# Moving two elementwise passes of a backward pass's last phase to GpSimd and its running sums to ScalarE

## The chip, the cores and the metric

The kernel runs on one core of a Trainium2 chip. The metric is the device time of one execution in microseconds (us). The kernel before takes 434.45 us, the median of three runs (434.1 to 438.83). Runs of one kernel wander by about 1%, so each kernel below is compared with runs of the kernel before on the same chip, in the same rounds.

Names used throughout: PE is TensorE, DVE is VectorE, ACT is ScalarE, POOL is GpSimd, SP is SyncE, which issues the DMAs. L1231 is line 1231 of the kernel's source. The change has one line less than the kernel before, so the same statement can carry a number one lower there.

## The reference, cut to what matters

A transformer block with a spectral mixing layer (a 2D FFT filter) and a squared-ReLU MLP, both behind a modulated layer norm, is run forward and backward in bf16. All gradients are outputs.

```python
def _layernorm(x, axis=-1, eps=1e-05):
    m = jnp.mean(x, axis=axis, keepdims=True)
    v = jnp.var(x, axis=axis, keepdims=True)
    return (x - m) / jnp.sqrt(v + eps)
# ... in the forward function:
    h = _layernorm(x, axis=-1) * (1 + ca) + sa
    x = x + ga * _A_ref(h, A_w_r, A_w_i)          # spectral layer
    h = _layernorm(x, axis=-1) * (1 + cb) + sb
    x = x + gb * _B_ref(h, B_w1, B_b1, B_w2, B_b2) # MLP
# ... and jax.vjp of it for the gradients
```

The last phase computes the gradient through the first layer norm for 2048 rows of 512. For a row with normalised value n and incoming gradient h, it needs h\*n summed over the rows (for the modulation), and two sums along the row, of s and of s\*n, where s is the scaled gradient. Beside that, TensorE still computes the gradient of the MLP's second weight.

## The kernel before

The 2048 rows are 16 tiles of 128, taken in 8 pairs. One pair does this:

```python
def row_pair(t, Ts):
    n1, gxl = rows3[t]                      # loaded from DRAM, two buffers each
    ...                                     # gh1, q1: three buffers; gn, gs, rr: two
    for i in range(2):
        psY = spec_g3(tc, K, Ts[i], psE)    # PE
        nc.scalar.copy(out=gs[:, i, :], in_=psY)                       # L1226
    unfold(nc, fp, gh1, gs, 2, "unf_u")     # four DVE passes, L261 to L265
    nc.vector.tensor_tensor(gn, gh1, modb[:, CA1_B, None, :].broadcast_to([P, 2, D]), op=ALU.mult)  # L1228
    for i in range(2):
        nc.scalar.activation(gs[:, i, :], gn[:, i, :], AF.Copy, scale=inv1[...], accum_out=rr[:, i, 0:1])  # L1230
    nc.vector.tensor_tensor(q1, gh1, n1, op=ALU.mult)                  # L1231
    late.add(lambda: colsums1(t, gh1, q1))  # PE sums over rows, L1212, 4 to 7 us after q1 in the trace, under 2 us for the last two pairs
    for i in range(2):                      # product and running sum in one, L1235
        jk = fp.tile([P, D], BF16, name="jk1", bufs=1)
        nc.vector.scalar_tensor_tensor(out=jk, in0=gs[:, i, :], scalar=K["onef"], in1=n1[:, i, :],
                                       op0=ALU.mult, op1=ALU.mult, accum_out=rr[:, i, 1:2])
    nc.vector.tensor_scalar(rr[:, :, 2:4], rr[:, :, 0:2], -1.0 / D, None, op0=ALU.mult)   # L1237
    for i in range(2):
        nc.vector.tensor_scalar(gn[:, i, :], n1[:, i, :], rr[:, i, 3:4], rr[:, i, 2:3], ...)  # L1239
    nc.vector.tensor_tensor(gs, gn, gs, op=ALU.add)                    # L1240
    gx = fp.tile([P, 2, D], BF16, name="gx")
    nc.vector.tensor_tensor(gx, gs, gxl, op=ALU.add)                   # L1242
    nc.sync.dma_start(out1_view[:, t:t + 2, :], gx)
    load_rows3(t + 4)
```

Between the pairs stand units of the weight gradient, each 16 matmuls, an evacuation from PSUM on DVE, an output, and a transposing load for a later unit:

```python
def grad_w2(fc):
    ps = mmps.tile([P, SB], FP32, name="mm")
    for t in range(NT):
        nc.tensor.matmul(ps, lhsT=hns[fc][:, t, :], rhs=g_sb[:, t, :], ...)   # L1150
    gw = gwp.tile([P, D], BF16, name="gw", bufs=3)
    with tc.high_priority():
        nc.vector.tensor_tensor(gw, ps, modb[:, GB_B, :], op=ALU.mult)        # L1153
    nc.sync.dma_start(out6_view[:, fc, :], gw)
    load_hn()                                                                 # L1145, transposing
```

## Time and profile before

| | before |
|---|---|
| time, median | 434.45 us |
| span of the profiled run | 436.5 us |
| row phase: start of the first unfold pass to end of the last gx | 358.94 to 424.80, 65.9 us |
| DVE busy in the row phase | 57.3 us |
| PE gaps longer than 0.1 us, from the first unfold to the last matmul | 7.4 us |
| GpSimd work in the row phase | none |

The row phase is the stage to read. The share of a whole run says little about it: from 359 to 425 PE is busy for 58.63 and DVE for 57.47 of 66 us, the DMA share is 1.03, and GpSimd is idle. The prediction shows the lines.

### The profile page before, as it was taken

To read this page: it belongs to the slowest core of one execution; us is meant where nothing else is said; L and a number is where in the kernel's file an instruction comes from. 1 tells how busy PE (TensorE), PEld (TensorE's weight loads), DVE (VectorE), ACT (ScalarE), POOL (GpSimd) and SP (SyncE) were. 2 spreads that over 40 slices of the span, in tenths; PEclk is the share of its full clock that TensorE was granted. 3 is DMA by queue.
4 is the path that set the end of the run, shared out by engine and by line. 5 is a ranking of instruction groups with operands and counts; after the bars stand their busy time and mean duration, and the time that the engine had idled before them with its cause. 6 is when DMAs were issued, how large, how long until landed. Compare 5 with 4: busy or idle time off the path is not lost.

```text
span 436.5 us, 7027 instructions
## 1 busy us (share of the span) xinstructions
PE 398.5 (91%) x2353; PEld 195.4 (45%) x2375; DVE 351.4 (80%) x846; ACT 261.2 (60%) x493; POOL 13.0 (3%) x64
## 2 busy tenths in 40 slices
PE   2789989999999999999999999999899799993996
PEld 0335446654444434443444444455455464441332
DVE  6887758959997588969897998909686968978896
ACT  5797889769881286348536765365348375445331
POOL 6120000000000000000000000000000000000000
PEclk9998999999999999999999999999999999999899
DMA  8995779999298469669965997987995699999984
GB/s 240 238 291 146 188 290 267 279 311 256 91 379 245 136 114 352 165 165 229 270 195 153 222 338 267 211 204 229 273 300 158 168 253 259 222 260 244 275 235 144
DMA packets 149738, 101.09 MB, mean 232 GB/s; under 512 B 98753, under 2 KB 135494, under 8 KB 149062
## 3 DMA queue, kind: packets, MB, share of 16 engines
q1 hardware_dynamic: 149138, 100.12, 86.6%
q10 hardware_dynamic: 564, 0.53, 0.4%
q8 instruction: 18, 0.29, 0.3%
q14 instruction: 18, 0.15, 0.1%
HBM read 35.44 MB, written 41.60 MB: 176 GB/s over the span
## 4 chain that ended last, share of the span: by engine, by line
PE 35%; DVE 28%; DMA 14%; ACT 12%; SPq 5%; issue 5%; POOL 1%; ACTq 0%; DVEq 0%
PE og L880 10%; PE mm L853 6%; PE mm L694 4%; PE mm L1150 4%; DMA n<-n_dram 3%; DMA out_dram<-gw 2%; DMA x<-in_A_x_dram 2%; DVE gm_junk L465 2%; PE psG L341 2%; SPq L1145 2%; PE mod_ps L595 2%; PE mm L1081 2%; DMA n_dram<-x_sb 2%; DVE l_st L795 1%; ACT r L855 1%
## 5 line engine op out<-in xcount | busy, mean ns | idle before, releaser
L694 PE MATMUL mm<-gT,w2T 128*128 128x512 bf16 x224 | 58.1, 383 | 3.4 <-DVE gab L697 2.7
L853 PE MATMUL mm<-h2T,w 128*128 128x512 bf16 x224 | 53.6, 379 | 1.7 <-ACT r L855 1.5
L1150 PE MATMUL mm<-g_sb,hn 128*128 128x512 bf16 x217 | 51.6, 387 | 3.8 <-DVE gw L1153 3.4
L1081 PE MATMUL mm<-gab,h_sb 128*128 128x448 bf16 x256 | 51.5, 352 | 2.5 <-ACT gw L1085 2.5
L880 PE MATMUL og<-w1T,gab 128*128 128x512 bf16 x218 | 49.9, 379 | 1.1 <-DVE o L945 0.8
L880 PE MATMUL og<-w,h 128*128 128x512 bf16 x217 | 49.1, 379 | 0.3
L855 ACT ACTIVATE r<-mm,b1col 128x512 bf16<-128x512 f32 x56 | 37.0, 684 | 6.1 <-PE mm L853 3.7
L1081 PEld LDWEIGHTS <-h_sb 128*128 128x128 bf16 x256 | 24.6, 98 | 24.2 <-issue 3.6
L853 PEld LDWEIGHTS <-w 128*128 128x128 bf16 x224 | 21.1, 97 | 30.6 <-issue 8.8
L1150 PEld LDWEIGHTS <-hn 128*128 128x128 bf16 x224 | 21.3, 99 | 29.8 <-issue 7.1
L880 PEld LDWEIGHTS <-h 128*128 128x128 bf16 x224 | 21.8, 98 | 26.1 <-issue 0.9
L880 PEld LDWEIGHTS <-gab 128*128 128x128 bf16 x224 | 21.6, 98 | 25.9 <-issue 1.4
L694 PEld LDWEIGHTS <-w2T 128*128 128x128 bf16 x224 | 20.9, 98 | 23.1 <-issue 6.5
L893 ACT CAST G<-og 128x512 bf16<-128x512 f32 x16 | 9.2, 580 | 27.9 <-PE og L880 27.9
L699 ACT CAST gab<-mm 128x512 bf16<-128x512 f32 x36 | 21.7, 602 | 3.0 <-PE mm L694 2.9
L857 DVE TENSOR_TENSOR h<-r 128x1024 bf16<-128x1024 bf16 x28 | 19.2, 687 | 4.8 <-ACT r L855 4.8
L1085 ACT CAST gw<-mm 128x448 bf16<-128x448 f32 x16 | 8.7, 543 | 24.0 <-DMA out_dram<-gw 15.0
L1230 ACT ACTIVATE gs<-gn,inv 128x512 bf16<-128x512 bf16 x16 | 11.4, 716 | 18.3 <-DVE gn L1228 18.3
L413 DVE TENSOR_TENSOR p<-Z,G 128x1028 bf16<-128x1028 bf16 x8 | 5.6, 697 | 19.9 <-DMA Xb<-xs_dram 11.6
L372 ACT ACTIVATE Tsb<-psT 128x512 bf16<-128x512 f32 x32 | 18.5, 604 | 1.6 <-PE psT L370 1.6
L465 DVE SCALAR_TENSOR_TENSOR gm_junk<-wmc,onef,gmbc 128x512 bf16<-128x512 bf16 x24 | 17.9, 747 | 1.9 <-DMA wmc<-in_w_mod_dram 1.0
L697 DVE CAST gab<-mm 128x512 bf16<-128x512 f32 x20 | 13.7, 686 | 6.8 <-PE mm L694 6.7
(287 smaller groups left out, 757.1 us busy)
## 6 DMA issues: line engine op xcount, KB each, us to landing
h_dram<-h SPq DMA_DIRECT2D x28, 256.0 KB, 3.6
gh_dram<-gab SPq DMA_DIRECT2D x28, 256.0 KB, 3.8
w<-in_B_w_dram SPq DMA_DIRECT2D x2, 1792.0 KB, 7.7
wmc<-in_w_mod_dram SPq DMA_DIRECT2D x12, 256.0 KB, 4.7
out_dram<-gwm SPq DMA_DIRECT2D x12, 256.0 KB, 3.7
wz_dram<-Z SPq DMA_DIRECT2D x8, 258.0 KB, 2.4
xs_dram<-Xs SPq DMA_DIRECT2D x8, 258.0 KB, 3.2
Z<-wz_dram SPq DMA_DIRECT2D x8, 258.0 KB, 4.3
```

What stands on the lines that cost most here:

```text
L372: nc.scalar.activation(Tsb, ps, AF.Copy, scale=EF_S)
L465: nc.vector.scalar_tensor_tensor(out=junk, in0=wmc[:, i, :], scalar=K["onef"], in1=gmbc, op0=ALU.mult, op1=ALU.mult, accum_out=self.gsc[:, ...
L694: nc.tensor.matmul(ps, lhsT=w2T[:, dc, fc * P:(fc + 1) * P], rhs=gT[b][:, :, dc, :], start=(dc == 0), stop=(dc == 3))
L697: nc.vector.tensor_copy(out=gaT[b][:, fc, :], in_=ps)
L699: nc.scalar.copy(out=gaT[b][:, fc, :], in_=ps)
L853: nc.tensor.matmul(ps, lhsT=w1[:, dc, (fc + i) * P:(fc + i + 1) * P], rhs=h2T[b][:, :, dc, :], start=(dc == 0), stop=(dc == 3))
L855: nc.scalar.activation(r[:, i, :], ps, AF.Relu, bias=b1col[:, fc + i:fc + i + 1])
L857: nc.vector.tensor_tensor(h2, r, r, op=ALU.mult)
L880: nc.tensor.matmul(ps, lhsT=lhs(fc), rhs=rhs[:, fc, :], start=(fc == 0), stop=(fc == NFC - 1))
L1081: nc.tensor.matmul(ps[:, 0:W4], lhsT=h2_sb[:, t, dc * P:(dc + 1) * P], rhs=ghn[t // 4][:, t % 4, fs], start=(t == 0), stop=(t == NT - 1))
L1150: nc.tensor.matmul(ps, lhsT=hns[fc][:, t, :], rhs=g_sb[:, t, :], start=(t == 0), stop=(t == NT - 1))
L1230: nc.scalar.activation(gs[:, i, :], gn[:, i, :], AF.Copy, scale=inv1[:, t + i:t + i + 1], accum_out=rr[:, i, 0:1])
```

## The change

The intent is to unload DVE. Two passes go to idle GpSimd. The sum of s\*n, a fused product and sum on DVE, becomes a plain product on DVE and an accumulating copy on ScalarE.

```diff
-            nc.vector.tensor_tensor(q1, gh1, n1, op=ALU.mult)
+            nc.gpsimd.tensor_tensor(q1, gh1, n1, op=ALU.mult)
             late.add(lambda: colsums1(t, gh1, q1))
+            nc.vector.tensor_tensor(gn, gs, n1, op=ALU.mult)
             for i in range(2):
-                jk = fp.tile([P, D], BF16, name="jk1", bufs=1)
-                nc.vector.scalar_tensor_tensor(out=jk, in0=gs[:, i, :], scalar=K["onef"], in1=n1[:, i, :], op0=ALU.mult, op1=ALU.mult,
-                                               accum_out=rr[:, i, 1:2])
+                nc.scalar.activation(gn[:, i, :], gn[:, i, :], AF.Copy, accum_out=rr[:, i, 1:2])
 ...
-            nc.vector.tensor_tensor(gx, gs, gxl, op=ALU.add)
+            nc.gpsimd.tensor_tensor(gx, gs, gxl, op=ALU.add)
```

## The prediction

"Port" and "lock" are words for a supposition: GpSimd and DVE hold each other up when both work in SBUF. No large GpSimd pass is in the trace before, so this and the duration of such a pass were supposed, and the "overhang" (the time by which the work of both engines would exceed the phase), the +5 us taken from it and the 81 us of the second rival were the author's estimates, shown by no trace at that time.

> **What bounds the kernel now.** I began with the page's busy shares, to see which engine has room for moved work.
>
> ```profile
> PE 398.5 (91%) x2353; PEld 195.4 (45%) x2375; DVE 351.4 (80%) x846; ACT 261.2 (60%) x493; POOL 13.0 (3%) x64
> ```
>
> TensorE is busy for 91% of the span. GpSimd is idle after the set-up, which invites the change. But the edit touches only the last phase, so that stage decides. The timeline puts the row pairs there: the first unfold starts at 358.94 us and the last output add (L1242) ends at 424.80. I asked for the busy time in four stretches: the whole phase, its start, its middle, and the rest up to the end of the matmuls. The columns are stretch, its length, then busy us and instruction counts of PE, PEld, DVE, ACT, POOL, then granted clock, DMA share and GB/s.
>
> ```profile
> 359.00:425.00 66.00, 58.63 (x318) 25.18 (x323) 57.47 (x138) 30.28 (x68) 0.00 (x0) 0.97 1.03 245
> 359.00:390.00 31.00, 30.67 (x182) 14.55 (x187) 28.06 (x68) 17.10 (x40) 0.00 (x0) 1.00 1.04 232
> 390.00:403.00 13.00, 6.22 (x46) 2.50 (x40) 8.94 (x20) 4.74 (x11) 0.00 (x0) 1.00 1.03 264
> 403.00:433.00 30.00, 29.19 (x126) 11.37 (x128) 27.61 (x72) 10.37 (x21) 0.00 (x0) 0.94 0.89 238
> ```
>
> Three resources are nearly full at once: PE 89%, DVE 87% and the DMA engines at a share of 1.03. Before 390 and after 403, PE is at 97 to 99%, and its work is not changed. The only PE time to win lies in 390 to 403: 13.00 - 6.22 = 6.78 us, 1.6% of 434.45. So even a perfect relief of DVE can hardly pass 2%.
>
> What causes this hole? The waits of 359 to 433 (waiting line, released by, total us, times, longest):
>
> ```profile
> ACT gs L1230 <- DVE gn L1228: 18.3, 6, 4.4
> ACT gs L1226 <- DVE gx L1242: 12.3, 3, 5.4
> ...
> DVE q L1231 <- DMA n<-n_dram: 6.2, 3, 3.1
> ...
> PE mm L1060 <- DVE gn L1239: 3.5, 1, 3.5
> PE mm L1150 <- DVE gw L1153: 3.4, 1, 3.4
> ```
>
> The two PE waits sum to 6.9 us and are the hole. The chain of work that ended last shows what lay behind it:
>
> ```profile
> 388.68 3.98 DMA n<-n_dram
> 392.66 0.02 issue
> 392.68 0.07 DVE q L1231
> ...
> 394.56 0.08 DVE jk L1235
> 394.65 0.06 DVE gx L1242
> 394.71 0.46 issue
> 395.17 0.68 DVE gw L1153
> ...
> 397.83 3.95 DMA n<-n_dram
> ```
>
> DVE executes in order. It stands for 3.1 us at L1231 until a late load of n1 lands, and the PSUM evacuation gw (L1153) stands behind it, so PE has nowhere to write. The n1 load is late because one SyncE queue issues, in order, the outputs, the row loads and the transposing loads of hn (median 3.1 us each in the queue). The second wait in the list matters too: ScalarE's L1226 cannot refill gs before gx (L1242) of two pairs earlier has read it.
>
> [...]
>
> **The change part by part.** DVE operations follow each other by less than their duration (starts of equal 128x1024 passes are 0.60 us apart for a duration of 0.68), so I count occupied time:
> - Off DVE: q1 (L1231), 8 x 0.60 = 4.8 us; gx (L1242), 8 x 0.60 = 4.8; the fused product and sum (L1235), 16 x (0.67 + 0.08 for reading the accumulator) = 12.0. Sum 21.6.
> - On DVE: one plain product gs*n1 into gn per pair, 8 x 0.60 = 4.8. Net -16.8 us: from 57.5 to about 40.7 us in the 66.
> - On ScalarE: 16 accumulating copies. Two successive L1230 start 0.71 us apart including the accumulator read; [...] But each pair's chain gains a hop, DVE product to ACT sums to DVE L1237, where before DVE went straight on.
> - [...]
>
> [...] I take about half of the overhang: +5 us. There is also latency: [...] L1226 already waited for gx three times. SyncE is held longer at the output of gx, and the n1 loads stand behind it. One thing gets better: q1's wait for n1 leaves DVE; but the new product reads n1 as well, so DVE only meets that wait one ScalarE step later. The consumer of q1, the column sums (L1212), runs about 3 to 5 us after q1 for most pairs (pair 3: q1 at 384.21, sums at 388.99)[...].
>
> Sum: 434.45 + 5 = 439.5 us, +1.2%.
>
> **Rivals.**
> 1. GpSimd does not disturb DVE much. Then DVE has 40.7 us of work in 66, gw is never late except by the n1 wait, and part of PE's 6.8 us closes. For it: PE and DVE are both near full, so any freed DVE time shortens the wait of gw. Against: the hole starts with a DMA, at a DMA share of 1.03, which no elementwise edit relieves. I would expect 2 to 5 us won: 429 to 432.
> 2. The port serialises fully, and a blocked GpSimd pass makes gx and q1 late. [...] the phase takes about 81 us instead of 66: 434.45 + 15 = 449 us. For it: DVE's sequence is dense with two-input operations. Against: ScalarE waits already leave gaps for the port.
> 3. The wait of DVE on its own port is mild, but gx's late output holds SyncE's queue. It waited 15 us in all for buffers of hn in this phase (8.1 + 3.7 + 3.3), so about 1.9 us a pair can be absorbed. [...] the transposes of hn begin to starve PE: 436 to 442 us.
> 4. All is hidden behind PE, which is 97% busy outside the hole: 434 us, within 0.5%.
>
> **Range and chances.** The PE bound caps the gain at 6.8 us, so under 427.7 is hardly to be had; faster by 2% means under 425.8. I give it 0.08, for effects of a new order of instructions that I do not see. Rivals 1, 3 and 4 and my own sum all land within 2% (425.8 to 443.1). The full lock lands beyond it. The port's behaviour is the large unknown, so I leave much weight there: slower 0.39, same 0.53. The range, 8 in 10: 429 to 452 us.
>
> **What the profile will show.** If I am right: 16 GpSimd tensor_tensor passes whose starts, back to back, are 2.2 to 2.6 us apart [...]; DVE two-input passes in the phase with a mean well above 0.68 us, or with gaps before them, only when GpSimd runs; gw unstretched in itself but late; ACT waiting for gx from GpSimd instead of DVE; the distance from the first unfold to the last gx about 71 us instead of 66; PE idle in the phase above 7.4 us. DVE operations that keep 0.68 us beside GpSimd would show the lock wrong, and rival 1 or 4 holds. A GpSimd pass much faster than 2 us, or a hole at 390 to 403 that closes, would make the prediction too high; SyncE waiting long at the output of gx with starved hn loads would be rival 3.

## The result, and the profile after

The change takes 451.69 us (median of 4 runs, 450.12 to 454.65) against 435.54 us of the kernel before (4 runs). The ratio is 1.0368, with a 95% interval of 1.028 to 1.0455: clearly slower. A ratio here is the mean time of one kernel's fast runs over that of the other's of the same rounds, so it is not quite the ratio of the quoted medians.

The spans of the two profiled runs differ by 448.4 - 436.5 = 11.9 us. The difference splits without a remainder. The first unfold pass starts at 356.30 instead of 358.94 (2.6 us earlier, before anything was changed). The row phase takes 78.9 instead of 65.9 us (+13.0). What follows the last gx takes 13.2 instead of 11.7 us (+1.5).

Busy time in stretches of the changed kernel, columns as in the prediction; the first line is its row phase:

```profile
356.30:435.20 78.90, 63.45 (x309) 26.95 (x313) 66.44 (x97) 40.80 (x100) 36.97 (x16) 0.87 0.92 205
...
390.00:403.00 13.00, 9.69 (x63) 4.17 (x62) 11.25 (x18) 7.33 (x19) 5.54 (x3) 1.00 1.02 212
403.00:433.00 30.00, 22.31 (x89) 8.45 (x91) 25.00 (x39) 14.41 (x35) 12.36 (x6) 0.77 0.69 159
```

DVE's busy time was to fall and has risen, from 57.3 to 66.4 us, with 41 instructions fewer (97 for 138). Its idle time has risen too, from 8.5 to 12.5 us. PE, which was busy for 29.19 of the 30 us from 403 to 433, is now busy for 22.31. The DMA share has fallen to 0.92, so the DMA engines do not bind more than before.

Which DVE work has grown? Groups by line, first of the kernel before, then of the changed one (busy us, mean ns of one, idle before):

```profile
L1228 DVE TENSOR_TENSOR gn<-gh,modb 128x1024 bf16<-128x1024 bf16 x8 | 5.5, 688 | 0.1
...
L262 DVE TENSOR_TENSOR unf_u<-gs 128x512 bf16<-128x512 bf16 x8 | 3.4, 419 | 0.0
```

```profile
L1153 DVE TENSOR_TENSOR gw<-mm,modb 128x512 bf16<-128x512 f32 x14 | 9.6, 684 | 2.8 <-PE mm L1150 2.8
L1228 DVE TENSOR_TENSOR gn<-gh,modb 128x1024 bf16<-128x1024 bf16 x8 | 8.7, 1089 | 0.2
...
L262 DVE TENSOR_TENSOR unf_u<-gs 128x512 bf16<-128x512 bf16 x8 | 7.2, 897 | 0.0
```

The same pass on the same data takes a mean of 897 ns instead of 419, and 1089 instead of 688. The evacuation L1153, with one input from PSUM, kept its 0.68 us. Summed over the groups that grew (count times the growth of the mean), DVE was stretched by 23.7 us: L1228 3.2, the new product 5.6 (against the 688 ns of a like pass), the unfold passes L261, L262 and L264 1.9, 3.8 and 3.7, the two tensor_scalar groups 1.8 each, and L465 of the tail 1.9.

One place of the timeline shows how (start, duration, engine, line; in brackets the engine's idle time before and what ended it; other engines left out):

```profile
368.35 0.69 DVE L1228 TENSOR_TENSOR gn<-gh,modb 128x1024 bf16<-128x1024 bf16 x1
368.40 2.63 POOL L1231 TENSOR_TENSOR q<-gh,n 128x1024 bf16<-128x1024 bf16 x1 [1.41 <-DVE gh L265]
...
368.96 2.34 DVE L261 TENSOR_TENSOR unf_u<-gs 128x512 bf16<-128x512 bf16 x1
...
371.23 0.41 DVE L262 TENSOR_TENSOR unf_u<-gs 128x512 bf16<-128x512 bf16 x1
```

L1228 starts first and runs its normal 0.69 us. The GpSimd pass starts behind it and lasts 2.63 us; undisturbed ones last 2.12. Then the DVE pass L261, normally 0.42 us, lasts 2.34 us: it ends at 371.30, with the GpSimd pass (371.03). Here the engines take turns, and each waits inside its own recorded duration (2.34 us on DVE, 2.63 us on GpSimd). That is why the loss shows as DVE busy time.

The chain of work that ended last shows the same within its own pieces (start, us, what), where the chain before showed late DMAs:

```profile
417.35 2.20 DVE gn L1228
...
421.66 2.07 DVE gn L1233
...
423.77 0.61 PE acc L1212 x3
424.38 5.94 PE mm L1150 x17
```

Two stretched DVE products stand in the chain before the last column sums, and PE's remaining matmuls only start then. The chain follows inferred releasers, though, and cuts L1233 off at 423.73, before its end at 424.27. By the list of waits the sums stood last for q1, the GpSimd pass from 421.15 to 423.72:

```profile
PE acc L1212 <- POOL q L1231: 2.9, 2, 2.3
```

The order on PE differs too: 81 recorded matmuls follow the last column sums, where 57 did before the change, so more work stood behind this wait. The share of either in the loss was not isolated; the junk products below, which nobody waits for, cost as much with the old order.

PE gaps have grown from 7.4 to 15.1 us. After one of them PE's granted clock drops:

```profile
373.80:376.30 2.50, 0.02 (x1) 0.00 (x0) 2.48 (x2) 0.85 (x4) 1.34 (x1) 1.00 1.35 51
376.30:381.70 5.40, 5.30 (x16) 1.99 (x16) 4.34 (x8) 2.98 (x11) 2.12 (x1) 0.68 1.10 222
```

A gap of 2.5 us is followed by 16 matmuls that take 5.30 us at a mean clock of 0.68, where 16 took 3.62 us in the kernel before (at 376.30). In steps of 0.5 us the clock is still 1.00 until about 377.5, then 0.50 until about 380.8, then 1.00 again. Not every gap is followed by this: in the kernel before, the matmuls after a gap of 3.48 us (394.48 to 397.96) ran at 1.00, and only those after the next gap of 3.40 us at 0.52. PE's busy time is 404.6 instead of 398.5 us. Whether this is a cause of the loss is asked below.

### The profile page after: what moved, and what is told of

Its sections match the earlier page's.

```text
span 448.4 us, 7057 instructions
## 1 busy us (share of the span) xinstructions
PE 404.6 (90%) x2353; PEld 197.3 (44%) x2375; DVE 360.9 (80%) x806; ACT 271.7 (61%) x525; POOL 49.9 (11%) x80
## 5 line engine op out<-in xcount | busy, mean ns | idle before, releaser
L1150 PE MATMUL mm<-g_sb,hn 128*128 128x512 bf16 x217 | 55.9, 414 | 3.5 <-DVE gw L1153 2.8
L1150 PEld LDWEIGHTS <-hn 128*128 128x128 bf16 x224 | 23.3, 106 | 33.4 <-issue 13.3
L853 PEld LDWEIGHTS <-w 128*128 128x128 bf16 x224 | 21.1, 97 | 30.6 <-issue 8.8
L1231 POOL TENSOR_TENSOR q<-gh,n 128x1024 bf16<-128x1024 bf16 x8 | 19.8, 2472 | 117.7 <-ACT gs L1230 107.0
L1230 ACT ACTIVATE gs<-gn,inv 128x512 bf16<-128x512 bf16 x16 | 11.4, 714 | 16.8 <-DVE gn L1228 16.8
L465 DVE SCALAR_TENSOR_TENSOR gm_junk<-wmc,onef,gmbc 128x512 bf16<-128x512 bf16 x24 | 19.7, 822 | 1.3 <-ACT gmbc L454 0.7
```

The lines of the kernel that those rows point to most:

```text
L465: nc.vector.scalar_tensor_tensor(out=junk, in0=wmc[:, i, :], scalar=K["onef"], in1=gmbc, op0=ALU.mult, op1=ALU.mult, accum_out=self.gsc[:, ...
L853: nc.tensor.matmul(ps, lhsT=w1[:, dc, (fc + i) * P:(fc + i + 1) * P], rhs=h2T[b][:, :, dc, :], start=(dc == 0), stop=(dc == 3))
L1231: nc.gpsimd.tensor_tensor(q1, gh1, n1, op=ALU.mult)
```

## The experiments

Three theories stood at the start. **Port**: GpSimd's passes and DVE's two-input passes exclude each other, as the collision at 368.96 suggests (L261 takes 2.34 us instead of 0.42); the name stands for whatever the two share. **Late**: the passes are just slower on GpSimd, so q1 and gx come late and hold buffers and the output queue. **Hop**: the sums on ScalarE lengthen each pair's chain.

### The parts of the change alone

Only the sums on ScalarE (the change with both passes back on DVE):

```diff
-            nc.gpsimd.tensor_tensor(q1, gh1, n1, op=ALU.mult)
+            nc.vector.tensor_tensor(q1, gh1, n1, op=ALU.mult)
-            nc.gpsimd.tensor_tensor(gx, gs, gxl, op=ALU.add)
+            nc.vector.tensor_tensor(gx, gs, gxl, op=ALU.add)
```

> Three theories of the +16 us. [...] LATE: gx and q1 arrive later from GpSimd, so gs and the output queue are held. HOP: the new product and ScalarE sums lengthen each pair's chain. This run keeps only the sums on ScalarE, both passes stay on DVE. PORT and LATE: no loss; DVE sheds 16 x 0.75 - 8 x 0.60 = 7.2 us, so 429 to 436 us and DVE passes at their old 0.42 and 0.69 us. HOP: most of the loss is here, 445 to 452 us.

Measured: 435.67 us against 436.89, ratio 0.999 (0.9964 to 1.0016). Row phase 65.4 us. Hop is refuted. The relief of DVE is real (its busy time is 346.3 instead of 351.4 us) but buys nothing, as the hole in PE stays (gaps 7.8 us).

Only the two passes on GpSimd (the kernel before with q1 and gx moved):

```diff
-            nc.vector.tensor_tensor(q1, gh1, n1, op=ALU.mult)
+            nc.gpsimd.tensor_tensor(q1, gh1, n1, op=ALU.mult)
-            nc.vector.tensor_tensor(gx, gs, gxl, op=ALU.add)
+            nc.gpsimd.tensor_tensor(gx, gs, gxl, op=ALU.add)
```

> Both passes on GpSimd, the sums on DVE as before. PORT: at least as slow as the whole change, since DVE keeps 7.2 us more work [...]: 450 to 462 us, DVE passes stretched to over 2 us. LATE: 445 to 452 us, with DVE passes unstretched. HOP: 433 to 438 us.

Measured: 452.32 us, ratio 1.0371 (1.0309 to 1.0434); row phase 80.2 us. The two passes carry the whole loss.

Only q1, then only gx on GpSimd (one of the two edits each):

> Only q1 on GpSimd, 8 passes. Its result is wanted 3 to 5 us later by the column sums. PORT: the port is held 8 x 2.2 = 18 us for 4.8 us off DVE: about half of the loss of both passes, 439 to 446 us. LATE: nothing hangs closely on q1, 432 to 437 us. HOP: 433 to 437 us.

> Only gx on GpSimd, 8 passes. gs, gxl and the output queue wait for it. PORT: like q1 alone, within some 4 us of it, 439 to 447 us. LATE: nearly the whole loss is here, 446 to 452 us, and far slower than q1 alone. HOP: 433 to 437 us.

Measured: q1 alone 443.09 us, ratio 1.0157 (1.01 to 1.0214), row phase 70.7 us; gx alone 444.8 us, ratio 1.0187 (1.0137 to 1.0236), row phase 72.4 us. Both are clearly slower than before; whether by more than 2% is unclear for each. The excesses add up: 1.57 + 1.87 = 3.44% against 3.71% for both. Late had put nearly all on gx, since the column sums want q1 only later. Port had put about half on each, and so it is.

### Take the waiting for gx away

The whole change, but pairs from the third on get their own gs, in rows of a tile that is no longer needed:

```diff
-            gs = fp.tile([P, 2, D], BF16, name="gs")
+            gs = fp.tile([P, 2, D], BF16, name="gs") if t < 4 else h2_sb[:, t:t + 2, :]
```

> The whole change, but from the third pair on each pair has its own gs, in rows no longer needed, so ScalarE's copy L1226 never waits for gx on GpSimd (7.6 us of waits, 3 times). PORT: little changes, 446 to 453 us. LATE: the loss shrinks by half or more, below 444 us.

Measured: 452.14 us, ratio 1.0356 (1.0301 to 1.0412), row phase 78.5 us. The waits of L1226 for gx are gone from the list (7.6 us before this edit), and the time has not moved. Late is refuted as the main cause as far as gx holds gs; a late q1 is not tested here.

### GpSimd work that nobody waits for

The kernel before keeps all its DVE work and gets GpSimd products whose results are thrown away:

```diff
             nc.vector.tensor_tensor(q1, gh1, n1, op=ALU.mult)
+            nc.gpsimd.tensor_tensor(h2_sb[:, 0:2, :], gh1, modb[...], op=ALU.mult)
             ...
             nc.vector.tensor_tensor(gx, gs, gxl, op=ALU.add)
+            nc.gpsimd.tensor_tensor(h2_sb[:, 0:2, :], gx, modb[...], op=ALU.mult)
```

> The kernel before, all its DVE work kept, plus 16 GpSimd products (of gh1, then of gx, with a row of modb) into rows that nobody reads any more. No result of GpSimd is waited for by the chain; only the buffers of gh1 (three) and gx come free later. PORT: 16 x 2.2 = 35 us of port time against DVE, nothing saved: 448 to 462 us, with DVE passes over 2 us. LATE and HOP: 434 to 439 us, DVE passes at 0.42 and 0.69 us.

Measured: 462.33 us, but one output was wrong (relative error 0.125 in the first MLP weight's gradient). The rows that I overwrote were still read by two of its units in program order, which also moved those units behind the junk on PE. The run proves nothing. Two more kernels had the same fault and are told below. The clean form makes the junk only from the second pair on (`if t >= 2`), 14 products; PE's order of work is then that of the kernel before.

> The junk products again, now only from the second pair on (14 passes), when the rows they overwrite are surely unused: the first form delayed and spoiled part of the weight gradient and moved TensorE's order, so its 462 us proved nothing. Order on TensorE is as before and the result must be correct. PORT: 14 x 2.2 = 31 us of port time, no DVE work saved: 446 to 460 us, with DVE two-input passes over 2 us. LATE or HOP: 434 to 439 us.

Measured: correct, 451.92 us against 433.38, ratio 1.042 (1.0395 to 1.0446), row phase 80.3 us. DVE's groups:

```profile
L1237 DVE SCALAR_TENSOR_TENSOR jk<-gs,onef,n 128x512 bf16<-128x512 bf16 x16 | 17.7, 1107 | 0.3
L1231 DVE TENSOR_TENSOR q<-gh,n 128x1024 bf16<-128x1024 bf16 x8 | 14.0, 1756 | 0.9 <-DMA n<-n_dram 0.9
...
L1153 DVE TENSOR_TENSOR gw<-mm,modb 128x512 bf16<-128x512 f32 x14 | 9.5, 681 | 0.4 <-PE mm L1150 0.3
```

The fused product and sum takes 1107 ns instead of 747, q1 on DVE 1756 instead of 687, and the evacuation with its single SBUF input is untouched. No result of GpSimd is waited for here, yet the loss is as large as the change's.

### GpSimd work that only writes

If the shared thing is a path for reads, a GpSimd instruction that only writes must spare the two-input passes. One element is copied to set the moment, then 128x2560 are filled:

```diff
+            nc.gpsimd.tensor_copy(h2_sb[:, 0, 0:1], gh1[:, 0, 0:1])
+            nc.gpsimd.memset(h2_sb[:, 0:5, :], 0.0)
```

(and the same after gx). In the expectations of these two runs, 434 to 440 and 434 to 442 us are the forecasts of Port if only reads by GpSimd hold up DVE's two-input passes. That the fill holds tensor_scalar was only supposed before the first; before the second, the first form had shown 0.66 instead of 0.41 us. The first form, with the fault just told:

> As the junk products, but GpSimd only writes: one element is copied to set the moment, then a fill of 128x2560, meant to last about 2 us. [...] PORT by reading: 434 to 440 us, two-input passes unstretched at 0.42 and 0.69 us, at most L1239 longer than 0.41. If any GpSimd work hurts (issue, semaphores, memory): 446 us and more.

Measured: 445.82 us, ratio 1.0207, one output wrong; not used for a verdict on time. The clean form:

> The write-only junk in the same clean form: 14 times one element copied and 2.2 us of fill. Its first form showed two-input passes near 0.69 us and bf16 tensor_scalar (L1239 before) at 0.66 instead of 0.41 us. [...] 434 to 442 us, clearly below the junk products of the same call. If any GpSimd activity hurts alike: within 3 us of the junk products.

Measured: correct, 436.06 us, ratio 1.0058 (1.0038 to 1.0078), row phase 66.6 us. The fills last 2.2 us each, like the products, and cost a seventh of what they cost (0.58% against 4.2%). A place of its timeline where both kinds of DVE work meet a fill:

```profile
400.36 2.23 POOL L1234 MEMSET h_sb<- 128x2560 bf16 x1
...
400.90 0.42 DVE L261 TENSOR_TENSOR unf_u<-gs 128x512 bf16<-128x512 bf16 x1
...
401.24 1.38 DVE L1240 TENSOR_SCALAR rr<-rr 128x4 f32<-128x4 f32 x1
...
401.31 1.31 DVE L262 TENSOR_TENSOR unf_u<-gs 128x512 bf16<-128x512 bf16 x1
```

The two-input pass L261 runs in the middle of the fill in its normal 0.42 us. The tensor_scalar on only four columns (normally 0.16 us) is held until the fill is over, at 402.62, and L262 only because it stands behind it. Over the whole run L261 has a mean of 420 ns and the fused product and sum 747 ns, as in the kernel before, while that tensor_scalar has one of 989 ns instead of 162 (up to 1.92 us).

### Is there a version that beats both?

The prediction had laid the hole in PE at 390 to 403 to late loads of n1. So the rows of the last four pairs were loaded earlier, into unused rows, without GpSimd:

```diff
-            load_rows3(t + 4)
+            if t < 4:
+                load_rows3(t + 4)
+            with tc.issue_after(od.ins):   # behind this pair's output
+                load_rows3(t + 8)          # lands in h2_sb
```

> The kernel before, without GpSimd and with its sums on DVE; rows n1 and gxl of the last four pairs are loaded up to two pairs earlier, into rows no longer needed. If the hole of 6.8 us of TensorE at 390 to 403 comes from the late n1 loads behind the transposing loads, it closes in part: 428 to 434 us against before. If DVE (87% busy) or the DMA share above 1 is the true bound there, no gain: 434 to 438 us.

Measured: 445.23 us, ratio 1.0183, one output wrong, by the same fault; not used. The clean form loads them from the second pair on (pairs 4 and 5 at t=2, pair 6 at t=4, pair 7 at t=6):

> The kernel before with rows n1 and gxl of the last four pairs loaded earlier into rows no longer needed, now from the second pair on, so that nothing of the weight gradient is overwritten. If the hole of 6.8 us on TensorE comes from late n1 loads, DVE's waits for n1 (6.2 us) fall below 2 us and the time to 428 to 434 us at a before of 436.8. If DVE's load or the DMA share binds there: 435 to 438 us.

Measured: 435.69 us against 433.38, ratio 1.0042 (1.002 to 1.0064): the same within 2%, and slower rather than faster. The waits for n1 fell from 6.2 to 1.4 us as meant, but two PE waits are as long as ever, and DVE now stands in front of something else:

```profile
DVE gw L1153 <- DMA out_dram<-gw: 5.6, 2, 4.5
...
PE mm L1150 <- DVE gw L1153: 3.5, 1, 3.5
PE mm L1060 <- DVE gw L1153: 3.5, 1, 3.5
```

The evacuation waits for its output buffer, whose DMA is late. The chain there reads SyncE's transposing load (3.17 us), then that output (3.54 us). So n1 was only the first transfer to suffer; another takes its place.

The early rows with the sums on ScalarE (both edits together):

> The early rows together with the sums on ScalarE, no GpSimd. If DVE's 7.2 us of relief had no effect alone because the n1 loads bound the middle, it pays here: 426 to 432 us, 1 to 4 us below the early rows alone. If TensorE and DMA bound the rest: equal to the early rows alone.

Measured: 435.15 us, ratio 1.0043 (1.0025 to 1.0062). DVE's relief does not pay here either. No version tried beats the kernel before; the sums alone equal it.

## Why the prediction was right or wrong

**The small prize** was right: DVE relief alone is worth nothing (sums alone: 0.999).

**The direction** leaned right: the central forecast was slower by 1.2%, the odds for slower by over 2% were only 0.39, and it came out slower by 3.7%. The time lies at the top of the range (451.69 of 452). Two of the four runs lie above it, so that the median fell inside is partly luck.

**The GpSimd duration** measured 2.12 us undisturbed by its span, about 3.1 times the 0.68 us of the same pass on DVE. By the spacing that the prediction had asked for, and for which it forecast 2.2 to 2.6 us, junk products that follow each other at once start 2.20 us apart. ScalarE's new copies took 621 ns, against 716 of L1230 in the kernel before.

**The lock**, at first supposed only, was right and is now shown, by junk reads (1.042), junk writes (1.0058) and the single collisions (L261 2.34 us instead of 0.42 beside a GpSimd product, 0.42 inside a fill). What it is that the engines share is not shown.

**The step that failed is a size**: "I take about half of the overhang: +5 us". The row phase grew by 13.0 us instead of 5, DVE busy by 9.1 us and DVE idle by 3.9 us. Of the two terms behind the +5, one came out. The prediction's 71 us for the phase stood, as estimate, for the work of DVE and GpSimd less what lies side by side; measured, DVE is busy for 66.4 us and GpSimd works another 4.4 us while DVE is idle, 70.8 us together. Of the 37 us of GpSimd time, 23.7 us reappeared as stretched DVE work, more than the relief of 16.8 us that was counted. Only 3.0 us lay beside evacuations, since DVE executes in order and an evacuation behind a blocked pass is blocked with it, though its own duration stays at 0.69 us (L1153 at 367.30 starts when L264, held for 2.22 us, has ended).

The other term failed: DVE's 8.5 us of idle time were counted as room that the new demand fills. Instead DVE is idle for 12.5 us, and for 8.1 us of these GpSimd does not work either. Most of the 12.5 us are waits for ScalarE:

```profile
DVE rr L1236 <- ACT gn L1235: 5.8, 6, 1.4
...
DVE gn L1233 <- ACT gs L1230: 3.8, 3, 1.7
```

Why this time was not used stays open. DVE idles for 13.7 us of the row phase with own buffers for gs and for 10.2 us with the passes alone, but for only 1.9 us with the junk products, whose results nobody waits for. So by this account work makes up 5 of the 13 us and idle time the other 8; whether the lock brings about that idle time too, through later starts along each pair's chain, was not tested.

**The rivals**: the full lock came nearest in numbers (449 us and a phase of 81 us, measured 451.69 and 78.9); its phase, an estimate, was the only one with waits on top of the work (4.5 us for n1). Its second half, late gx and q1, is not needed for a loss of this size: own buffers for gs changed nothing, and the junk products cost as much. But PE did wait 2.9 us for q1, and that share was not isolated. The rival of SyncE held by gx showed 2.7 us of waits in all, with a lower DMA share, so it is minor. The harmless rivals fell.

**The cause of the hole** was told too simply. The n1 load was its releaser, but removing that wait left the hole. What sets it, the order of SyncE's queue or the DMA engines' load, is open.

**PE's clock** I had not foreseen. It is shown to drop after some gaps (to 0.50 after the one of 2.5 us), but it is not needed for the loss: the passes alone have larger PE gaps (21.1 against 15.1 us), less time at the lowered clock (PE busy 400.4 against 404.6 us), and the same time. Its own share was not isolated.

## What to carry to other kernels

Before moving a pass to idle GpSimd, ask what DVE does meanwhile: if DVE's passes read two SBUF tensors, a moved pass takes much of its 2.1 us from DVE (here 23.7 of 37 us), for 0.7 us of DVE time saved each. In such a profile the loss hides in DVE's busy time, so compare the mean duration of unchanged groups before and after. Count an in-order engine's unblocked work as blocked when it stands behind blocked work (L1153 behind L264's 2.22 us), do not book its idle time as free room (here 8.5 us of it became 12.5), and check that the engine relieved is the one that the end waits for.
